# Moving one block of VectorE work and splitting one exponential in a fused attention and feed-forward kernel

## The chip, the cores and the metric

The kernel runs on one core of a Trainium2 chip. The metric is device time in microseconds (us); of each kernel several executions are timed and the median is given. One execution is recorded by the hardware profiler; its rows are what the text quotes. The engines are TensorE (PE in the profile, its weight loads PEld), VectorE (DVE), ScalarE (ACT), GpSimd (POOL) and SyncE (SP). SP issues most transfers between memory and the chip's buffers, among them transfers that transpose. Every engine works through its own instructions in order and waits on semaphores for those of the others.

## The reference

Inputs are `x` (8 batches, 8 heads, 512 positions, 64 wide), `state` (8, 8, 32, 64) and two matrices, 512 by 2048 and 2048 by 512. For each batch and head:

```python
scores  = x @ state.T / 8;   a  = softmax(scores)      # over 32 states
xread   = a @ state
scores2 = state @ x.T / 8;   a2 = softmax(scores2)     # over 512 positions
sread   = a2 @ x
attn    = concat([xread, sread])                        # 544 rows
h = attn (all heads side by side, 4352 rows of 512) @ w_in
out = max(0.01 * h, h) @ w_out
```

The sums of both softmaxes get 1e-9 added. Input and output are fp32.

## The kernel before

**Tiling.** The kernel goes batch by batch, 0 to 7. All eight heads of a batch are one tile: the scores stand as 128 partitions (4 pairs of heads times 32 states) by 2 times 512 positions, in a PSUM tile of two banks called "sc". Most products run on bf16 copies. Instead of `a @ state @ w_in` the kernel forms `M = state @ w_in` once per batch, in four column blocks (`a_m(a, c, tag)` makes block c on PE in the PSUM tile named by `tag`, `m_evict` copies it to `a.M`), so that the first feed-forward layer is one product of the probabilities with M.

**A batch's first softmax** on the engines: `a_scores` (PE), then on DVE `a_max` (L266, maximum over the 32 states) and the two steps of `a_diff`: the maxima are spread over a tile `sh` (L274) and the scores less the maxima overwrite it (L280). `a_exp` (ACT, L284) writes the exponentials to `e1`. `a_recip` (DVE: L289 sums, L293 and L296 give the reciprocal, L298 spreads it) and `a_probs` (L302) give the probabilities `aT`.

**The second softmax** of the same scores: `a_max2` (DVE, L331), `a_exp2` (ACT, L337, for each half g, with the sums collected on the way in `r2`), `a_probs2` (DVE: L345 adds 1e-9, L347 the reciprocal, L355 two multiplications to bf16, one for each half). For batches 0 and 1 the result goes into a common tile `a2p`; a transfer on SP transposes it (`a_a2t_pair`, L373), and `a_sread` on PE multiplies it with x later, in batch 2's stage.

**The feed-forward layers.** `ff1(a, hT, s)`, s from 0 to 15, is a step: two matmuls into a bank of the tag "ph" (two banks in turn), then relu s on ACT (L437). A step's bank is free again for step s + 2 once relu s is done. The second layer of a batch runs as `piece`s between the steps: for batches 0 and 1 `piece(b, hT, i, jq)` adds four matmuls to the output block i, `y_store` (L547) copies a finished block out of PSUM with ACT or DVE and sends it off by SP (L548). From batch 1's second half on, products are replaced by sums of blocks and fewer products (a Strassen-like scheme): `tw_sum` forms combinations of w_out (L576), `s_sum` (L597) and `two_sum` (L673) those of h; `two_product` (L689, tile `ppr`) and `product` (L632) multiply.

**Order.** The order on every engine is written out by hand; the program text is the order of issue. The loop `for s in range(16)` with `ff1(a1, h1, s)` is batch 1's stage. Before it stands a prologue with batch 0's rest: there `a_exp2(a0)` is issued, `a_scores(a1)`, `a_shift(a1)` (maximum, spread, subtraction), `a_max2(a1)`, `a_exp(a1)`, the casts and transposing transfers of x for batch 2 (`cast_x`, L126, and `a_xt_half`, L240), the probabilities of batch 1, the cast and transposing transfer of the state for batches 2 and 3 (L209, L214), two `tw_sum`s of DVE (with `j` 0 and 4), `a_probs2(a0)`, and eight `tw_sum`s and a cast on POOL.

Two output blocks of batch 0 (i = 2 and 3) stand in a two-bank PSUM tile, `pyw`, of the tag "big". In step 1 of batch 1's stage their last matmuls run, and ACT copies block 2 and DVE block 3. In step 3, after `a_scores(a2)`, `a_m(a1, 3, "big")` writes into the same two banks (`pm`, L411), ACT evicts it, and DVE does `a_shift(a2)` and `a_max2(a2)`. In step 7 `a_exp(a2)` follows relu 7 on ACT; in step 9 `a_exp2(a2, 0)` follows relu 9, and on DVE come `a_recip(a2)` and `a_probs(a2)`; in step 11 `a_exp2(a2, 1)` and `a_probs2(a2)`; in step 13 `a_probs2(a1)`, an eviction of M of batch 2 by DVE (L425) and four `two_sum`s, with two more in step 0 of batch 2's stage. In step 1 of batch 2's stage `m_spread` (L1113) evicts one block of M from two banks, "ph" with ACT and "py" with DVE; the first `two_product` in step 2 takes that "py" bank after it.

Of the kernel before, what the change touches and what calls it, by code (L numbers as in the profile page):

```python
# [9 lines left out]
P = 128  # L10
B, H, S, D = 8, 8, 512, 64
# [8 lines left out]
BF16 = mybir.dt.bfloat16  # L20
FP32 = mybir.dt.float32
AF = mybir.ActivationFunctionType
ALU = mybir.AluOpType
# [4 lines left out]
def kernel(  # L28
# [9 lines left out]
    nc = tc.nc  # L38
# [4 lines left out]
    att = ctx.enter_context(tc.tile_pool(name="att", bufs=2))  # L43
# [10 lines left out]
    NB = 2 * S // NS  # L54
# [144 lines left out]
    def load_state(i):  # L199
        lo, hi = groups[i]  # L200
        for k in range(NK):
            for g in range(2):
                nc.sync.dma_start(
                    stf[i][NS * k:NS * (k + 1), :, D * g:D * (g + 1)],
                    state[lo:hi, 2 * k + g].rearrange("b n d -> n b d"),
                )
# [45 lines left out]
    def a_scores(a):  # L252
        sc = psum.tile([P, 2, S], FP32, name="sc", tag="sc", bufs=1)
        for k in range(NK):
            for g in range(2):
                nc.tensor.matmul(
                    sc[NS * k:NS * (k + 1), g, :],
                    lhsT=st_of(a, g, k),
                    rhs=a.xTh[k // 2][D * g:D * (g + 1), :, k % 2, :],
                    start=True, stop=True,  # L260
                )
        a.sc = sc

    def block_max(flat, n):
        m1 = att.tile([P, n], FP32, name="mrow", tag="mrow")
        nc.vector.tensor_reduce(  # L266
            out=m1[:], in_=flat.rearrange("p (c j) -> p c j", j=NS),
            axis=AX.X, op=ALU.max, apply_transpose=True,
        )
        return m1  # L270

    def block_spread(m1, n):
        sh = att.tile([P, n * NS], FP32, name="sh", tag="sh", bufs=1)
        nc.vector.transpose(  # L274
            sh[:].rearrange("p (c j) -> p c j", j=NS), m1[:, :, None].to_broadcast([P, n, NS])
        )
        return sh

    def block_diff(flat, sh):
        nc.vector.tensor_tensor(out=sh[:], in0=flat, in1=sh[:], op=ALU.subtract)  # L280

    def block_exp(sh, n):
        e1 = att.tile([P, n * NS], BF16, name="e1", tag="e1", bufs=1)
        nc.scalar.activation(out=e1[:], in_=sh[:], func=AF.Exp)  # L284
        return e1
# [21 lines left out]
    def a_max(a):  # L307
        a.flat = a.sc[:].rearrange("p g c -> p (g c)")
        a.m1 = block_max(a.flat, NB)

    def a_diff(a):
        a.sh = block_spread(a.m1, NB)
        block_diff(a.flat, a.sh)

    def a_shift(a):
        a_max(a)
        a_diff(a)

    def a_exp(a):
        a.e1 = block_exp(a.sh, NB)  # L320

    def a_recip(a):
        a.q1b = block_recip(a.e1, NB)

    def a_probs(a):
        a.aT = att.tile([P, 2, S], BF16, name="aT", tag="aT")
        block_probs(a.aT[:], a.e1, a.q1b)

    def a_max2(a):
        a.m2 = att.tile([P, 2], FP32, name="mcol", tag="mcol")  # L330
        nc.vector.tensor_reduce(out=a.m2[:], in_=a.sc[:], axis=AX.X, op=ALU.max, negate=True)  # L331

    def a_exp2(a, g):
        if g == 0:
            a.e2 = att.tile([P, 2, S], BF16, name="e2", tag="e2")
            a.r2 = att.tile([P, 2], FP32, name="r2", tag="r2")
        nc.scalar.activation(  # L337
            out=a.e2[:, g], in_=a.sc[:, g, :], func=AF.Exp,
            bias=a.m2[:, g:g + 1], accum_out=a.r2[:, g:g + 1],
        )  # L340
# [3 lines left out]
    def a_probs2(a):  # L344
        nc.vector.tensor_scalar(out=a.r2[:], in0=a.r2[:], scalar1=1e-9, scalar2=None, op0=ALU.add)  # L345
        q2 = att.tile([P, 2], FP32, name="qc", tag="qc")
        nc.vector.reciprocal(q2[:], a.r2[:])  # L347
        if a.b in (0, 6):
            pairs[a.b] = att.tile([P, 2, 2, S], BF16, name="a2p", tag="a2p", bufs=1)
        if a.b in (0, 1, 6, 7):  # L350
            a.a2 = pairs[a.b - a.b % 2][:, a.b % 2]
        else:
            a.a2 = att.tile([P, 2, S], BF16, name="a2", tag="a2", bufs=1)[:]
        for g in range(2):
            nc.vector.tensor_scalar(  # L355
                out=a.a2[:, g, :], in0=a.e2[:, g, :],
                scalar1=q2[:, g:g + 1], scalar2=None, op0=ALU.mult,
            )
# [60 lines left out]
    def m_evict(a, c, pm, copy):  # L419
        cols = slice(DM * c, DM * (c + 1))  # L420
        if isinstance(pm, list):
            for g in range(2):
                copy(a.M[:, g, cols], pm[g][:])
        else:
            copy(a.M[:, :, cols], pm[:])  # L425
# [3 lines left out]
    def ff1(a, hT, j):  # L429
        ph = psum.tile([P, S], FP32, name="ph", tag="ph")  # L430
        for g in range(2):
            nc.tensor.matmul(  # L432
                ph[:], lhsT=a.M[:, g, P * j:P * (j + 1)],
                rhs=a.aT[:, g, :],
                start=(g == 0), stop=(g == 1),
            )
        nc.scalar.activation(out=hT[:, j, :], in_=ph[:], func=AF.Prelu, scale=1 / SCALE, alpha=0.01)  # L437
# [93 lines left out]
    def piece(b, hT, i, jq, bank=None, copy=SCA, js=range(4)):  # L531
        if jq == 0 and js[0] == 0:
            y = ys[b, i] = Y()
            y.py = psum.tile([P, DM], FP32, name="py", tag="py")[:] if bank is None else bank
        y = ys[b, i]
        for j in [4 * jq + v for v in js]:
            nc.tensor.matmul(  # L537
                y.py, lhsT=hT[:, j, P * i:P * (i + 1)], rhs=w_out_bf[:, j, :],
                start=(j == 0), stop=(j == 15),
            )  # L540
        if jq == 3 and copy is not None:
            y_store(b, i, copy)

    def y_store(b, i, copy):
        tag = ("ysb", "s1", "ysb", "s6")[i]
        ysb = ypool.tile([P, DM], FP32, name="ysb", tag=tag, bufs=3 if tag == "ysb" else 1)
        copy(ysb[:], ys[b, i].py)  # L547
        nc.sync.dma_start(rows_of(b)[i], ysb[:])  # L548
# [18 lines left out]
    def tw_sum(n, j0, j1, eng):  # L567
        u, at = j0 // 4, slice(j0 % 4, j0 % 4 + j1 - j0)
        in0, in1 = {
            1: lambda: (w_block(0, 1, j0, j1), w_block(0, 0, j0, j1)),  # L570
            2: lambda: (w_block(1, 1, j0, j1), tw[1][u][:, at]),
            3: lambda: (w_block(1, 1, j0, j1), w_block(0, 1, j0, j1)),
            4: lambda: (w_block(1, 0, j0, j1), tw[2][u][:, at]),
        }[n]()
        with nc.allow_low_precision(reason="operands of bf16 products"):
            eng.tensor_tensor(out=tw[n][u][:, at], in0=in0, in1=in1, op=ALU.subtract)  # L576
# [185 lines left out]
    a0, a1, a2 = att_of[:3]  # L762
# [249 lines left out]
    m_evict(a1, 1, a_m(a1, 1, "ph"), SCA)  # L1012
    for i in (0, 1):
        piece(0, h0, i, 0, js=half[1])
    a_shift(a1)
    a_max2(a1)
    tw_open()
# [25 lines left out]
        piece(0, h0, i, 3, copy=None, js=half[0])  # L1043
    for j in (0, 4):
        tw_sum(2, j, j + 4, nc.vector)
    a_probs2(a0)
    for n in (4, 3):
        for j in range(0, HJ, 2):
            tw_sum(n, j, j + 2, nc.gpsimd)
# [6 lines left out]
    for s in range(16):  # L1056
        ff1(a1, h1, s)
        if s in (1, 3):
            two = ((2, SCA), (3, VEC)) if s == 1 else ((0, SCA), (1, SCA))
            for i, copy in two:  # L1060
                piece(0, h0, i, 3, copy=None, js=half[1])
            for i, copy in two:
                y_store(0, i, copy)
        elif s % 2:
            piece(*fill[s // 2 - 2])
        if s == 3:
            a_scores(a2)
            m_evict(a1, 3, a_m(a1, 3, "big"), SCA)
            a_shift(a2)
            a_max2(a2)  # L1070
        elif s == 5:
            load_state(1)
        elif s == 7:
            a_exp(a2)
            a_open(att_of[3], 3)
            a_xt_dma(att_of[3])
        elif s in (9, 11):
            a_exp2(a2, s // 2 - 4)
            if s == 9:
                a_a2t_pair(0, (0,))  # L1080
                a_recip(a2)
                a_probs(a2)
            else:
                a_probs2(a2)
                load_x(4, nc.sync)
        elif s == 13:
            a_probs2(a1)
            a_a2t_pair(0, (1,))
            pm = [a_m(a2, 0, "big"), a_m(a2, 1, "sc")]
            m_evict(a2, 0, pm[0], SCA)  # L1090
            m_evict(a2, 1, pm[1], VEC)
            q1 = two_open(h1, 2 * P, ("S0", "S1"), "py")
            for n in (1, 2, 3):
                two_sum(q1, n, 0, 4, nc.vector)
            two_sum(q1, 3, 4, 8, nc.vector)
# [19 lines left out]
    for b in range(2, B):  # L1115
        hT = hpool.tile([P, 16, S], BF16, name="hT", tag="hT")
        hTs[b] = hT
        a = att_of[b]
# [192 lines left out]
```

## Time and profile before

| | us |
|---|---|
| median of 3 runs (203.39 to 203.48) | 203.41 |
| the profiled execution | 203.55 |
| its span in the profile | 201.8 |
| PE busy | 193.9 (96%) |
| DVE busy | 161.8 (80%) |
| ACT busy | 142.0 (70%) |
| POOL busy | 72.7 (36%) |

The clock that PE was granted is full throughout. The first number of a timeline row is its start in us from the span's start, the second its length; then come engine, source line, operation, output and input tile, the count if several are merged, and in brackets how long the engine had been idle before and what ended that. `PEld` is PE's weight load, `SPq` is SP's queue. Ends of matmuls are modelled, so rows of PE overlap a little; starts are what can be compared. In the table of groups a row has line, engine, operation, tiles and shapes, count, then total busy us and mean ns.

### The profile page before, as it was taken

The page shows a single profiled execution, that of the slowest core. Times are in us where ns is not written, and L with a number is a line of the kernel's source. Part 1 is how long each engine was busy: PE and PEld are TensorE (multiplying, and loading weights), DVE is VectorE, ACT ScalarE, POOL GpSimd, SP SyncE. Part 2 cuts the span into 40 slices and gives each one's busy share as a digit, 9 for nine tenths or more (in the row PEclk, how much of TensorE's full clock was granted, in tenths as well). Part 3 has the DMA queues.
Part 4 walks back from the last instruction along what each step waited for, and adds up shares of the span by engine and source line. Part 5 has one row for each costly group of instructions (what it writes and reads, how often), then busy time and mean ns, then how long its engine had stood idle before and what let it go on. Part 6 is the DMA issues. An engine that isn't in the chain of part 4 may idle for free.

```text
span 201.8 us, 4599 instructions
## 1 busy us (share of the span) xinstructions
PE 193.9 (96%) x1853; PEld 129.9 (64%) x1880; DVE 161.8 (80%) x240; ACT 142.0 (70%) x273; POOL 72.7 (36%) x76
## 2 busy tenths in 40 slices
PE   7899999799999999999999999999999999999993
PEld 3543444344477667776776767676767777799982
DVE  2766798999998989985999889898999945984712
ACT  3579647788889868866887779686868555757420
POOL 8914184990280274027400670054004600540000
PEclk9999999999999999999999999999999999999999
DMA  5999999697999723952382505220025302210115
GB/s 200 208 207 298 210 292 154 150 355 152 241 218 160 279 54 50 234 239 55 71 241 110 157 3 104 104 109 0 0 89 164 61 3 99 112 45 12 52 38 170
DMA packets 38773, 27.75 MB, mean 138 GB/s; under 512 B 24416, under 2 KB 35808, under 8 KB 38752
## 3 DMA queue, kind: packets, MB, share of 16 engines
q1 hardware_dynamic: 33584, 20.78, 38.7%
q0 software_dynamic: 4832, 6.29, 15.3%
q10 hardware_dynamic: 336, 0.39, 0.8%
q8 instruction: 14, 0.23, 0.5%
q14 instruction: 7, 0.06, 0.1%
HBM read 17.30 MB, written 8.91 MB: 130 GB/s over the span
## 4 chain that ended last, share of the span: by engine, by line
PE 76%; DMA 15%; POOL 3%; DVE 3%; issue 1%; ACTq 1%; ACT 0%; POOLq 0%; DVEq 0%
PE ph L432 21%; PE ppx L632 18%; PE ppb L632 15%; DMA x<-in_x_dram 7%; DMA w_out_bf<-in_moe_w_out_dram 7%; PE ppr L689 6%; PE pm L411 3%; PE py L537 3%; PE pf L510 3%; PE ppw L632 3%; PE psr L384 2%; POOL w_in_bf L145 2%; DVE a2p L355 1%; DMA out_dram<-ysb 1%; DVE tw L576 1%
## 5 line engine op out<-in xcount | busy, mean ns | idle before, releaser
L437 ACT ACTIVATE hT<-ph 128x512 bf16<-128x512 f32 x112 | 66.5, 604 | 24.8 <-PE ph L432 21.8
L597 POOL TENSOR_TENSOR S<-hT,S 128x512 bf16<-128x512 bf16 x24 | 32.1, 1358 | 83.2 <-DVE S L597 68.3
L432 PE MATMUL ph<-aT,M 128*128 128x512 bf16 x202 | 60.6, 379 | 0.1
L632 PEld LDWEIGHTS <-S 128*128 128x128 bf16 x384 | 37.0, 98 | 12.7 <-issue 0.9
L632 PEld LDWEIGHTS <-hT 128*128 128x128 bf16 x288 | 28.0, 98 | 11.1
L597 DVE TENSOR_TENSOR S<-hT 128x1024 bf16<-128x1024 bf16 x24 | 24.8, 1056 | 3.6 <-ACT hT L437 3.5
L432 PEld LDWEIGHTS <-M 128*128 128x128 bf16 x224 | 20.9, 98 | 8.4 <-issue 2.3
L632 PE MATMUL ppx<-tw,S 128*128 128x256 bf16 x160 | 20.8, 273 | 0.3
L537 PEld LDWEIGHTS <-hT 128*128 128x128 bf16 x96 | 9.1, 97 | 11.4 <-issue 1.1
L537 PE MATMUL py<-w_out_bf,hT 128*128 128x512 bf16 x61 | 15.7, 379 | 0.1
L729 DVE TENSOR_TENSOR ysb<-ppb,s 128x512 f32<-128x512 f32 x12 | 8.3, 692 | 6.5 <-PE ppb L632 6.5
L632 PE MATMUL ppb<-w_out_bf,hT 128*128 128x256 bf16 x96 | 12.4, 273 | 0.2
L632 PE MATMUL ppb<-tw,S 128*128 128x256 bf16 x96 | 12.4, 272 | 0.1
L632 PE MATMUL ppb<-w_out_bf,S 128*128 128x256 bf16 x96 | 12.3, 273 | 0.2
L425 ACT CAST M<-pm 128x1024 bf16<-128x1024 f32 x11 | 11.2, 1018 | 1.7 <-PE pm L411 1.7
L632 PE MATMUL ppx<-w_out_bf,hT 128*128 128x256 bf16 x80 | 11.2, 272 | 0.1
L337 ACT ACTIVATE e<-sc,mcol 128x512 bf16<-128x512 f32 x16 | 11.1, 701 | 0.0
L632 PE MATMUL ppx<-tw,hT 128*128 128x256 bf16 x80 | 10.4, 273 | 0.2
L576 POOL TENSOR_TENSOR tw<-w_out_bf 128x512 bf16<-128x512 bf16 x8 | 9.0, 1161 | 4.0 <-DMA w_out_bf<-in_moe_w_out_dram 4.0
L132 POOL CAST xb<-xl 128x2048 bf16<-128x2048 f32 x5 | 9.5, 1893 | 0.8 <-PE psr L384 0.8
L331 DVE TENSOR_REDUCE mcol<-sc 128x2 f32<-128x1024 f32 x8 | 9.7, 1213 | 0.0
L289 DVE TRANSPOSE_TENSOR_REDUCE r<-e 128x32 f32<-128x1024 bf16 x7 | 8.7, 1245 | 1.0 <-ACT e L284 0.7
(147 smaller groups left out, 324.7 us busy)
## 6 DMA issues: line engine op xcount, KB each, us to landing
out_dram<-ysb SPq DMA_DIRECT2D x11, 512.0 KB, 2.7
xl<-in_x_dram SPq DMA_DIRECT2D x5, 1024.0 KB, 6.1
out_dram<-ysb SPq DMA_DIRECT2D x9, 256.0 KB, 4.5
w_in_bf<-in_moe_w_in_dram POOLq DMA_DIRECT2D x4, 512.0 KB, 9.1
xf<-in_x_dram SPq DMA_DIRECT2D x4, 256.0 KB, 3.8
w_out_bf<-in_moe_w_out_dram POOLq DMA_DIRECT2D x4, 256.0 KB, 13.6
x<-in_x_dram POOLq DMA_DIRECT2D x2, 512.0 KB, 14.4
w_out_bf<-in_moe_w_out_dram POOLq DMA_DIRECT2D x2, 512.0 KB, 16.8
```

The lines of the kernel that those rows point to most:

```text
L132: nc.gpsimd.tensor_copy(xt[b][:].rearrange("p t h d -> p h t d"), xl[b][:].rearrange("p h (t d) -> p h t d", t=NT),)
L289: nc.vector.tensor_reduce(out=r1[:], in_=e1[:].rearrange("p (c j) -> p c j", j=NS), axis=AX.X, op=ALU.add, apply_transpose=True,)
L331: nc.vector.tensor_reduce(out=a.m2[:], in_=a.sc[:], axis=AX.X, op=ALU.max, negate=True)
L337: nc.scalar.activation(out=a.e2[:, g], in_=a.sc[:, g, :], func=AF.Exp, bias=a.m2[:, g:g + 1], accum_out=a.r2[:, g:g + 1],)
L425: copy(a.M[:, :, cols], pm[:])
L432: nc.tensor.matmul(ph[:], lhsT=a.M[:, g, P * j:P * (j + 1)], rhs=a.aT[:, g, :], start=(g == 0), stop=(g == 1),)
L437: nc.scalar.activation(out=hT[:, j, :], in_=ph[:], func=AF.Prelu, scale=1 / SCALE, alpha=0.01)
L537: nc.tensor.matmul(y.py, lhsT=hT[:, j, P * i:P * (i + 1)], rhs=w_out_bf[:, j, :], start=(j == 0), stop=(j == 15),)
L576: eng.tensor_tensor(out=tw[n][u][:, at], in0=in0, in1=in1, op=ALU.subtract)
L597: eng.tensor_tensor(out=part(n), in0=in0, in1=in1, op=op)
L632: nc.tensor.matmul(q[bank][v], lhsT=lhsT, rhs=w_of(n, j), start=q["open", bank] and j == 0, stop=j == 7, skip_group_check=True,)
L689: nc.tensor.matmul(q.bank[w], lhsT=lhsT, rhs=w_of(n, j), start=n in (1, 2, 5) and j == 0, stop=j == HJ - 1, skip_group_check=True,)
```

## The change

Two things are altered. First, `a_probs2(a0)` (four DVE instructions) is issued ahead of `a_shift(a1)` in the prologue instead of behind the two DVE `tw_sum`s. Second, in batch 1's stage `a_shift(a2)` becomes `a_max(a2)` and `a_diff_halves(a2)`: the subtraction is issued as two instructions, one for each half of 512 columns; and `a_exp(a2)` becomes two instructions of 512 columns, of which the first stays behind relu 7 and the second goes behind relu 9, ahead of `a_exp2(a2, 0)`. The numbers computed are the same.

```diff
     def block_diff(flat, sh):
-        nc.vector.tensor_tensor(out=sh[:], in0=flat, in1=sh[:], op=ALU.subtract)
+        nc.vector.tensor_tensor(out=sh, in0=flat, in1=sh, op=ALU.subtract)
...
+    def a_diff_halves(a):
+        a.sh = block_spread(a.m1, NB)
+        a.e1 = att.tile([P, 2 * S], BF16, name="e1", tag="e1", bufs=1)
+        for g in range(2):
+            block_diff(a.flat[:, S * g:S * (g + 1)], a.sh[:, S * g:S * (g + 1)])
+
+    def a_exp_half(a, g):
+        at = slice(S * g, S * (g + 1))
+        nc.scalar.activation(out=a.e1[:, at], in_=a.sh[:, at], func=AF.Exp)
...
     for i in (0, 1):
         piece(0, h0, i, 0, js=half[1])
+    a_probs2(a0)
     a_shift(a1)
     a_max2(a1)
...
     for j in (0, 4):
         tw_sum(2, j, j + 4, nc.vector)
-    a_probs2(a0)
     for n in (4, 3):
...
         if s == 3:
             a_scores(a2)
             m_evict(a1, 3, a_m(a1, 3, "big"), SCA)
-            a_shift(a2)
+            a_max(a2)
+            a_diff_halves(a2)
             a_max2(a2)
         elif s == 5:
             load_state(1)
         elif s == 7:
-            a_exp(a2)
+            a_exp_half(a2, 0)
             a_open(att_of[3], 3)
             a_xt_dma(att_of[3])
         elif s in (9, 11):
+            if s == 9:
+                a_exp_half(a2, 1)
             a_exp2(a2, s // 2 - 4)
```

More of the change, by code (lines that the diff above doesn't have):

```diff
@@ L312, in a_diff @@
         a.sh = block_spread(a.m1, NB)
-        block_diff(a.flat, a.sh)
+        block_diff(a.flat, a.sh[:])
     def a_shift(a):
```

## The prediction

> **What bounds the kernel now.** I read the page's busy table first, then the chain of work that ended last in order of time, then the timeline around the places that the change touches.
>
> ```profile
> PE 193.9 (96%) x1853; PEld 129.9 (64%) x1880; DVE 161.8 (80%) x240; ACT 142.0 (70%) x273; POOL 72.7 (36%) x76
> ```
>
> TensorE (PE) works 193.9 us, 96% of the span of 201.8. So the question for each edit is whether it opens or closes one of the few holes in PE's time. The profiled execution took 203.55 us, 1.75 outside its span; the median of the three runs is 203.41, so what the sum moves is taken off 203.41. In the chain, from 34.87 us:
>
> ```profile
> 34.87 1.27 DVE tw L576
> 36.14 1.05 DVE r L345
> 37.41 2.17 DVE a2p L355 x2
> 39.58 0.61 DVE ysb L547
> ```
>
> From 36.1 to 39.6 the chain runs through `a_probs2(a0)` on VectorE (DVE): add, reciprocal, two multiplications. Behind it on the same queue stands a copy of a finished output block out of PSUM (L547, `y_store(0, 3, VEC)`). The timeline shows who waits for that copy:
>
> ```profile
> 34.44 4.99 POOL L576 TENSOR_TENSOR tw<-w_out_bf,tw 128x512 bf16<-128x512 bf16 x4 [1.18 <-DVE tw L576]
> ...
> 35.64 1.18 SPq L214 DMA_TRANSPOSE st_t<-stb  x1
> ...
> 36.98 0.59 ACT L547 COPY ysb<-pyw 128x512 f32<-128x512 f32 x1 [0.21 <-PE pyw L537]
> ...
> 38.43 1.09 ACT L547 COPY ysb<-py 128x512 f32<-128x512 f32 x2
> 38.72 0.11 PEld L256 LDWEIGHTS <-st_t 64*32 64x32 bf16 x8 [0.55 <-DMA st_t<-stb]
> ...
> 39.50 0.68 DVE L547 COPY ysb<-pyw 128x512 f32<-128x512 f32 x1
> ...
> 40.23 0.41 PE L411 MATMUL pm<-w_in_bf,st 64*32 64x512 bf16 x8 [1.10 <-DVE ysb L547]
> ```
>
> PE finishes the scores of batch 2 (L256) and stands 1.10 us, until the copy has emptied the two-bank "big" tile that `a_m(a1, 3, "big")` writes. It is PE's one long hole behind the start.
>
> **Part 1, the block leaves its old place.** The copy needs the product of its rows, and is queued until ScalarE (ACT) has copied its sister block: 36.98 + 0.59 = 37.57. With the block gone DVE ends the second `tw_sum` at 34.87 + 1.27 = 36.14 and is free. The copy then runs from 37.6 to 38.3 (0.68 by its row), before PE arrives. On SP its output transfer, and the state loads queued behind that, go earlier by as much; their readers are a stage away. The block itself issues no transfer. What is late next is the scores themselves: they start when the transposed state has landed.
>
> ```profile
> DMA to landing us min/median/max: 3.0/3.0/3.0
> ```
>
> 35.64 + 3.0 = 38.64, the scores at 38.72; nothing in the change moves this transfer (next part). After the scores, `a_m` can follow as it does one stage later, where no one is waited for:
>
> ```profile
> 53.67 0.40 PE L256 MATMUL sc<-xT,st_t 64*32 64x512 bf16 x8
> 53.88 0.40 PE L411 MATMUL pm<-w_in_bf,st_t 64*32 64x512 bf16 x8
> ...
> 55.52 1.04 PE L689 MATMUL ppr<-w_out_bf,hT 128*128 128x256 bf16 x8
> ```
>
> That is 0.21 after the scores' start, so 38.93 instead of 40.23: PE gains 1.30. ACT's next work, the eviction of this product, comes free at about 39.45 (two copies from 38.43); it began 0.48 after `a_m`'s start before (40.71, below) and would be ready at 39.41. I take PE's lead as D = 1.25.
>
> **Part 1, the block at its new place.** It stands now behind the copies of x^T (L1008) and ahead of batch 1's maximum (L266).
>
> ```profile
> 23.05 1.40 DVE L1008 COPY xT<-pxt 128x1024 bf16<-128x1024 bf16 x2
> ...
> 23.21 0.25 ACT L337 ACTIVATION_READ_ACCUMULATOR e<-sc,mcol 128x1 f32 x1
> ...
> 24.51 0.41 PE L256 MATMUL sc<-xT,st 64*32 64x512 bf16 x8
> ...
> 24.99 1.25 DVE L266 TRANSPOSE_TENSOR_REDUCE mrow<-sc 128x32 f32<-128x1024 f32 x1 [0.55 <-PE sc L256]
> ...
> 26.11 4.50 POOL L576 TENSOR_TENSOR tw<-w_out_bf 128x512 bf16<-128x512 bf16 x4 [4.04 <-DMA w_out_bf<-in_moe_w_out_dram]
> ...
> 33.07 0.69 DVE L302 TENSOR_TENSOR aT<-e,qb 128x1024 bf16<-128x1024 bf16 x1
> 33.23 1.04 ACT L126 CAST xb<-xl 128x1024 bf16<-128x1024 f32 x1 [1.45 <-DMA xl<-in_x_dram]
> ...
> 35.05 1.03 PE L432 MATMUL ph<-aT,M 128*128 128x512 bf16 x4
> ```
>
> Its input is ready: the last exponential of batch 0 ends at 23.46. Price, from the two such blocks that stand back to back later:
>
> ```profile
> 48.83 0.16 DVE L345 TENSOR_SCALAR r<-r 128x2 f32<-128x2 f32 x1
> ...
> 49.76 0.16 DVE L345 TENSOR_SCALAR r<-r 128x2 f32<-128x2 f32 x1
> ```
>
> 49.76 - 48.83 = 0.93. DVE is free at 24.45 and has 0.55 of idle time, so the maximum moves from 24.99 to 25.4, 0.4 late. Queued behind it: batch 1's subtraction, exponential and sum. ACT's exponential and next eviction move 0.4, and the first cast of x for batch 2 with them, and its transpose on SP; the second cast waits anyway for its transfer (1.45 us before 33.23), and SP's second transpose and the state transpose behind it go by that one. The probabilities of batch 1 (L302) end at 33.76, then at 34.2; PE reads them at 35.05. The second `tw_sum` waited for a weight transfer until 34.87 and takes up the rest. POOL starts its sums (34.44) 0.3 later, but has no multiplications of DVE between them any more, which I count as even. Cost on PE: 0. The cover is 1.2 us wide; without it each 0.1 us costs 0.1.
>
> Here a rule can be weighed. At the old place the same block took from 36.06 to 39.50, 3.44 us, the add 1.05 instead of 0.16. POOL's sums ran all that time, and at the new place POOL is idle until 26.11. If the slowness travelled with the block, batch 1's maximum would come 2.9 late, its probabilities at 36.7, PE would stand 1.6 at 35.05, and D would be 1.25 - 1.6 = -0.35. The Trainium skill, "SBUF — State Buffer", section "Who interferes with whom", says that VectorE and GpSimd share a pair of ports under an exclusive lock and the one that comes second is blocked outright, and that a scalar multiplication out of SBUF may take that pair. By that rule the block costs 0.93 here, and the sum stays; by the other reading it is the last rival but one.
>
> **Part 2, two halves.** Around the exponential of batch 2 (all as before the change):
>
> ```profile
> 40.71 1.01 ACT L425 CAST M<-pm 128x1024 bf16<-128x1024 f32 x1 [1.18 <-PE pm L411]
> ...
> 42.31 1.04 PE L432 MATMUL ph<-aT,M 128*128 128x512 bf16 x4
> 42.65 1.22 DVE L280 TENSOR_TENSOR sh<-sc,sh 128x1024 f32<-128x1024 f32 x1
> 42.94 1.08 ACT L437 ACTIVATE hT<-ph 128x512 bf16<-128x512 f32 x2 [0.23 <-PE ph L432]
> ...
> 43.79 1.21 DVE L331 TENSOR_REDUCE mcol<-sc 128x2 f32<-128x1024 f32 x1
> ...
> 43.97 1.06 ACT L284 ACTIVATE e<-sh 128x1024 bf16<-128x1024 f32 x1
> 44.05 1.03 PE L432 MATMUL ph<-aT,M 128*128 128x512 bf16 x3
> ...
> 44.94 1.07 ACT L437 ACTIVATE hT<-ph 128x512 bf16<-128x512 f32 x2
> 45.06 1.25 DVE L289 TRANSPOSE_TENSOR_REDUCE r<-e 128x32 f32<-128x1024 bf16 x1
> ...
> 45.89 0.69 ACT L337 ACTIVATE e<-sc,mcol 128x512 bf16<-128x512 f32 x1
> ```
>
> DVE's chain started with batch 2's maximum, queued behind the copy (39.50 + 0.68). Freed of it, it goes by the scores: 38.72 + 0.48 (batch 1: scores at 24.51, maximum at 24.99) = 39.2, 0.9 earlier. Subtraction in halves: 1.22 for the whole; the nearest half-size row is DVE's copy out of PSUM at 0.68, so 1.22 to 1.36, ending near 43.0 (maximum and transpose take 2.55: 42.65 less 40.10, where the copy had ended); the row maxima (L331, 1.21) end near 44.2. Both halves are there before ACT wants them.
>
> The exponential is the costly part. Before, it ran whole ahead of relu 8 (43.97 to 45.03) and DVE's sum L289 followed at 45.06. Now only half is ahead, and the sum waits for the half that is behind relu 9. Size of a half, by the other exponential of 128x512:
>
> ```profile
> L337 ACT ACTIVATE e<-sc,mcol 128x512 bf16<-128x512 f32 x16 | 11.1, 701 | 0.0
> ...
> L836 ACT ACTIVATE e<-scn 128x512 bf16<-128x512 f32 x2 | 1.2, 597 | 1.6 <-PE scn L810 1.6
> ```
>
> ACT starts work every 0.49 when it has a queue (two relus from 44.94, next start 45.89: 0.48 each; 42.94 to 43.97: 0.51). Relu 8 needs its product: PE starts it at 44.05 - D, and a relu begins 0.63 after its product's start (42.31, 42.94, where ACT was idle). So relu 8 at 44.68 - D, relu 9 0.49 later, half 1 another 0.49 later, 0.60 long, and the sum 0.03 after it: 46.29 - D. With D = 1.25 that is 45.04: DVE's sum starts no earlier than before (45.06), though PE is 1.25 ahead, and DVE stands idle from 44.2 to 45.0. Relus 10 and 11 come about 0.3 late against PE, which has 0.3 to 0.4 to spare there (an estimate: relu 10 came behind the exponential of 45.89, near 46.55, and its bank is wanted again two steps of 1.74 us, 42.31 to 44.05, after 44.05, near 47.5); at most 0.1 is lost, and the next step has room for it.
>
> Now DVE's queue behind the sum, which ran without a hole before:
>
> ```profile
> 53.74 0.43 DVE L673 TENSOR_TENSOR Sr<-Sr,hT 128x512 bf16<-128x512 bf16 x1
> 54.38 0.69 DVE L1113 CAST M<-pm 128x512 bf16<-128x512 f32 x1 [0.22 <-PE pm L411]
> ```
>
> From 45.06 to 54.17 DVE is busy end to end (probabilities of batch 2, two second-probability blocks, an eviction, six sums); then 0.22 idle, then the eviction of its half of `m_spread` (L1113). PE's first product ppr (55.52) reuses that "py" bank and, by the program's semaphores, waits for this eviction. Before: 54.38 + 0.69 = 55.07, 0.40 to spare (0.05 for the signal). Now the eviction starts at 54.20 + (46.29 - D - 45.06) and PE goes on 0.74 later: 56.17 - D. So PE keeps 55.52 - (56.17 - D) = D - 0.65. With D = 1.25: **0.60 us**; the other 0.65 is a new stall of PE at L689. After that PE leads by 0.60 and DVE by about 0.2 or less; I expect DVE to catch up within batch 2's relus and the stages behind, where PE sets the pace (96% busy), to keep the 0.60. 203.41 - 0.60 = 202.8.
>
> Unknown sizes: half 1 between 0.49 (a start each) and 0.70 (the exponential L337 with its sum, 701 ns), the relus' rhythm 0.48 to 0.55, D 1.15 to 1.30: the gain is 0.35 to 0.80, my value by the rows nearest in form.
>
> **Rivals.**
> 1. The backlog doesn't bind: DVE finds 0.5 us or more in the nine behind the sum, or the sum starts earlier. Then PE keeps the whole D: 203.41 - 1.25 = 202.15. For it: PE's and ACT's lead brings the inputs of these nine earlier. Against it: none of them waited for an input before, so earlier inputs shorten nothing.
> 2. The hole closes only partly, because the copy is itself held by POOL's sums. If it lost 0.94 like the add did, it ends at 39.25, D = 0.95 and the gain is 0.30: 203.1, no change. Against: its row has 0.68 though POOL's sum ran at that time. The Trainium skill's "SBUF — State Buffer" page, same section, agrees: an instruction with at most one SBUF input outside the two-port modes doesn't take the pair.
> 3. Slower: the block keeps its 3.44 us at the new place. D = -0.35, gain -1.0: 204.4. It decides from a block of about 1.7 us on (0.55 idle and 1.2 cover). Against it: POOL idle, and 0.93 at 48.83.
> 4. The removal does nothing, as another wait (ACT's sister copy, the transfer) holds `a_m` until 40.2. D = 0, and the halves cost 0.65: 204.05. It is slower by more than 0.41 from D under 0.24 on.
>
> **How the numbers follow.** 0.2% is 0.41 us, about what a measurement of this kernel can tell from no change. Forecast (gain 0.35 to 0.80, so 202.6 to 203.05): 0.60, of which 0.09 under 0.41. Rival 1: 0.14. Rival 2 and other partial losses down to nothing: 0.14. Rivals 3 and 4: 0.06 each. Faster 0.51 + 0.14 = 0.65, same 0.09 + 0.14 = 0.23, slower 0.12. The range goes from rival 1 to no gain, 202.1 to 203.5; it leaves out the slower rivals.
>
> **What would show it.** PE's wait for L547 at 40 us gone, `a_m` right behind the scores near 38.9; the moved block about 0.93 us long at 24.4; batch 1's ff1 at 35.05 as before; DVE idle near 44.5 until half 1's end near 45.0; a new wait of PE for M L1113 of some 0.5 us near 54.4; POOL's sums at 34 to 39 shorter. Wrong if PE waits at 35 us (rival 3), if the hole stays (4), or if no wait at L689 appears (1).

## The result

The changed kernel takes 202.74 us (median of 7) against 203.39 us for the kernel before on the same chip (7 runs): a ratio of 0.9973, 95% interval 0.9961 to 0.9986. The forecast was 202.8, a gain of 0.60; the medians differ by 0.65. The ratio, which leaves out one slower execution of 207.68 us, puts the gain at 0.55, between 0.28 and 0.79. The profiled execution took 202.80, its span is 201.0 instead of 201.8.

The changed file is longer, so line numbers behind the change are shifted by about ten: relus are L447, steps of `ff1` L442, `a_m` L421, the output copy L557, `two_product` L699, `m_spread` L1126, the halves of the exponential L330.

The busy table of the page:

```profile
PE 194.4 (97%) x1853; PEld 130.3 (65%) x1880; DVE 159.9 (80%) x241; ACT 142.3 (71%) x274; POOL 72.6 (36%) x76
```

PE runs the same 1853 matmuls. Its busy time is 0.5 us longer, nearly all of it ahead of batch 1's scores (22.75 against 22.30); behind them, up to the first `two_product`, its idle time shrinks. The view of who PE waited for, from 24 to 62 us, has no line for the output copy any more (1.1 us before). One line is new:

```profile
PE ppr L699 <- DVE M L1126: 0.4, 1, 0.4
```

The timeline of the changed kernel at the places that the prediction followed (start, length, engine, line):

```profile
24.31 0.16 DVE L355 TENSOR_SCALAR r<-r 128x2 f32<-128x2 f32 x1
...
24.46 0.41 PE L256 MATMUL sc<-xT,st 64*32 64x512 bf16 x8
...
24.71 0.62 DVE L365 TENSOR_SCALAR a2p<-e,qc 128x512 bf16<-128x512 bf16 x2
...
25.24 1.24 DVE L266 TRANSPOSE_TENSOR_REDUCE mrow<-sc 128x32 f32<-128x1024 f32 x1
...
33.31 0.69 DVE L302 TENSOR_TENSOR aT<-e,qb 128x1024 bf16<-128x1024 bf16 x1
...
35.00 1.03 PE L442 MATMUL ph<-aT,M 128*128 128x512 bf16 x4
...
37.55 0.69 DVE L557 COPY ysb<-pyw 128x512 f32<-128x512 f32 x1 [1.16 <-ACT ysb L557]
...
38.64 0.41 PE L256 MATMUL sc<-xT,st_t 64*32 64x512 bf16 x8
...
38.87 0.40 PE L421 MATMUL pm<-w_in_bf,st 64*32 64x512 bf16 x8
...
42.55 0.62 ACT L330 ACTIVATE e<-sh 128x512 bf16<-128x512 f32 x1
42.72 1.03 PE L442 MATMUL ph<-aT,M 128*128 128x512 bf16 x3
...
44.33 0.63 ACT L330 ACTIVATE e<-sh 128x512 bf16<-128x512 f32 x1
...
44.99 1.25 DVE L289 TRANSPOSE_TENSOR_REDUCE r<-e 128x32 f32<-128x1024 bf16 x1 [0.88 <-ACT e L330]
...
53.67 0.42 DVE L683 TENSOR_TENSOR Sr<-Sr,hT 128x512 bf16<-128x512 bf16 x1
...
54.01 0.68 DVE L1126 CAST M<-pm 128x512 bf16<-128x512 f32 x1
...
54.75 1.03 PE L699 MATMUL ppr<-w_out_bf,hT 128*128 128x256 bf16 x8 [0.35 <-DVE M L1126]
```

The moved block runs from 24.31 to the next start at 25.24: 0.93 us instead of 3.44. PE reads batch 1's probabilities at 35.00 without a wait. The copy L557 is done at 38.24, and `a_m` follows the scores by 0.23 instead of 1.51. DVE's sum L289 nevertheless starts at 44.99, where it started before (45.06), 0.88 us idle in front of it, and at 54.75 PE meets the new wait, for DVE's half of `m_spread`.

All profiles begin with a stretch of loading that differs by up to 1.2 us between executions. To compare spans without it I take the time from batch 1's scores (the row at 24.46; 24.51 before) to the start of the last run of products. The chain of the changed kernel and of the one before end with these products:

```profile
188.21 6.13 PE ppr L699 x56
```

```profile
188.98 6.13 PE ppr L689 x56
```

188.21 - 24.46 = 163.75 against 188.98 - 24.51 = 164.47: 0.72 less. To the first ppr it is 54.75 - 24.46 = 30.29 against 31.01, also 0.72 less. So the whole gain is what is won at 39 us less what is lost at 54, and the 130 us behind keep it.

### The profile page after: what moved, and what is told of

Its sections match the earlier page's. It is cut to its first block, busy times and chain, and to the rows that moved or that the text cites. A ratio compares the mean times of both kernels' runs of the same rounds, so it can differ in the third digit from the quotient of the medians.

```text
span 201.0 us, 4601 instructions
## 1 busy us (share of the span) xinstructions
PE 194.4 (97%) x1853; PEld 130.3 (65%) x1880; DVE 159.9 (80%) x241; ACT 142.3 (71%) x274; POOL 72.6 (36%) x76
## 4 chain that ended last, share of the span: by engine, by line
PE 79%; DMA 8%; DVE 5%; POOL 3%; ACT 1%; issue 1%; ACTq 1%; POOLq 0%
PE ph L442 20%; PE ppx L642 18%; PE ppb L642 15%; DMA x<-in_x_dram 7%; PE ppr L699 6%; PE py L547 3%; PE pf L520 3%; PE pm L421 3%; PE pyw L547 3%; PE ppw L642 3%; PE psr L394 2%; POOL w_in_bf L145 2%; DVE Sr L683 1%; DMA out_dram<-ysb 1%; PE sc L256 1%
## 5 line engine op out<-in xcount | busy, mean ns | idle before, releaser
L447 ACT ACTIVATE hT<-ph 128x512 bf16<-128x512 f32 x112 | 66.6, 605 | 25.1 <-PE ph L442 22.1
L442 PE MATMUL ph<-aT,M 128*128 128x512 bf16 x202 | 60.7, 379 | 0.1
L442 PEld LDWEIGHTS <-M 128*128 128x128 bf16 x224 | 20.9, 98 | 8.7 <-issue 2.9
L289 DVE TRANSPOSE_TENSOR_REDUCE r<-e 128x32 f32<-128x1024 bf16 x7 | 8.7, 1245 | 1.4 <-ACT e L330 0.9
```

Of the source, the lines that this page charges most:

```text
L289: nc.vector.tensor_reduce(out=r1[:], in_=e1[:].rearrange("p (c j) -> p c j", j=NS), axis=AX.X, op=ALU.add, apply_transpose=True,)
L442: nc.tensor.matmul(ph[:], lhsT=a.M[:, g, P * j:P * (j + 1)], rhs=a.aT[:, g, :], start=(g == 0), stop=(g == 1),)
```

## The experiments

Each row of the table is a profile; "to ppr" is the start of the first `two_product` and "to the end" that of the last run of products, both counted from batch 1's scores. "Sum" is the start of DVE's sum L289, counted alike.

| kernel | sum | to ppr | to the end | against before | median, us (before on that chip) |
|---|---|---|---|---|---|
| before | 20.55 | 31.01 | 164.47 | | 203.41 |
| changed | 20.53 | 30.29 | 163.75 | -0.72 | 202.74 (203.39) |
| changed, again | 20.60 | 30.36 | 163.82 | -0.65 | 202.86 (203.42) |
| e1 move only | 19.65 | 29.94 | 163.41 | -1.06 | 202.44 (203.49) |
| e2 halves only | 21.82 | 31.58 | 165.04 | +0.57 | 204.17 (203.49) |
| e3 both halves behind relu 7 | 19.57 | 29.86 | 163.32 | -1.15 | 202.44 (203.49) |
| e4 two sums behind the subtraction | 20.68 | 29.92 | 164.79 | +0.32 | 203.86 (203.49) |
| e6 block under POOL's sums | 21.46 | 31.58 | 165.04 | +0.57 | 204.09 (203.42) |
| e7 two sums behind the maxima | 20.54 | 29.78 | 163.24 | -1.23 | 202.07 (203.42) |
| e7, again | 20.63 | 29.87 | 163.33 | -1.14 | 202.40 (203.43) |
| e8 second half behind relu 8 | 20.05 | 29.86 | 163.33 | -1.14 | 202.45 (203.42) |
| e9 whole exponential behind relu 9 | 21.10 | 30.85 | 164.32 | -0.15 | 203.17 (203.43) |
| e10 move and two sums, no halves | 19.77 | 30.06 | 163.53 | -0.94 | 202.46 (203.43) |

Two executions of the same kernel differ by 0.07 to 0.09 in this count, so steps of a tenth say nothing. Part of such a difference is the start of batch 2's scores, which wait for their transposed state: it lies 14.10 to 14.37 behind batch 1's in these profiles (15.02 in e6, where PE itself is late). The intervals of e2, e4 and e9 contain 1, so their times alone do not tell them from the kernel before; what is said of them rests on the traces.

### One part at a time: e1 and e2

e1 is the kernel before with the block moved and nothing else:

```diff
+    a_probs2(a0)
     a_shift(a1)
...
         tw_sum(2, j, j + 4, nc.vector)
-    a_probs2(a0)
```

> The block of second probabilities moved, nothing split. My theory (PE keeps its lead D less what DVE's queue behind the sum L289 lacks, and the halves only delay that sum): the whole exponential ends near 44.0, the sum starts near 44.1 instead of 45.0, DVE's half of m_spread ends 0.9 earlier, PE does not wait at its first ppr; relus 8 and 9 come 0.5 late and cost PE 0.1. Gain 1.1 to 1.2 against before: 202.2 to 202.3. Rival A (ACT binds: the whole exponential in front of relus 8 and 9 holds PE's steps 10 and 11 by 0.4 or more, which is what the split is for): 202.6 to 202.8, with a wait of PE for ph near 44.5. Rival B (the move alone is the whole effect and the split does nothing): same as the changed kernel, 202.7.

Measured: 202.44, ratio 0.9947 (0.9921 to 0.9974). The move alone gains more than the whole change, 1.06 against 0.72 in the count from batch 1's scores; the intervals of the two ratios overlap a little. Its timeline:

```profile
42.82 1.06 ACT L284 ACTIVATE e<-sh 128x1024 bf16<-128x1024 f32 x1 [0.26 <-DVE sh L280]
...
43.48 1.03 PE L537 MATMUL py<-w_out_bf,hT 128*128 128x512 bf16 x4
...
43.91 1.25 DVE L289 TRANSPOSE_TENSOR_REDUCE r<-e 128x32 f32<-128x1024 bf16 x1
43.96 1.89 POOL L132 CAST xb<-xl 128x2048 bf16<-128x2048 f32 x1
...
44.41 1.08 PE L432 MATMUL ph<-aT,M 128*128 128x512 bf16 x4
...
45.18 0.70 DVE L293 TENSOR_SCALAR r<-r 128x32 f32<-128x32 f32 x1
...
51.98 1.09 DVE L673 TENSOR_TENSOR Sr<-hT 128x512 bf16<-128x512 bf16 x3
...
53.45 0.68 DVE L1113 CAST M<-pm 128x512 bf16<-128x512 f32 x1
...
54.20 1.04 PE L689 MATMUL ppr<-w_out_bf,hT 128*128 128x256 bf16 x8
```

The exponential runs whole behind relu 7 and DVE's sum starts at 43.91, 0.9 earlier than in the changed kernel counted from the scores (19.65 against 20.53). PE does not wait at ppr: it starts at 54.20, 0.43 behind the row before it, as in the kernel before (55.52 - 55.09). It is a close thing, as DVE's half of `m_spread` ends only at 54.13. Rival A falls: PE's step at 44.41, which needs relu 8, comes 0.93 behind the row before it instead of 0.86, a loss of about 0.1 as the theory had it and not of 0.4. What I had not seen: of the 0.9 us half is lost again, as the small addition L293 behind the sum takes 0.70 instead of 0.18 while POOL's cast (43.96 to 45.85) runs.

e2 is the changed kernel with `a_probs2(a0)` back behind the two `tw_sum`s.

> The block at its old place, the subtraction and the exponential in halves. My theory: the hole of 1.1 us at 40 stays, the sum L289 starts near 46.3 instead of 45.06, DVE's half of m_spread ends near 56.1 and PE waits about 0.6 at its first ppr: slower by 0.65, 204.05. Rival (the split is free, as DVE catches up elsewhere): 203.4.

```profile
40.52 0.41 PE L421 MATMUL pm<-w_in_bf,st 64*32 64x512 bf16 x8 [1.02 <-DVE ysb L557]
...
46.61 1.25 DVE L289 TRANSPOSE_TENSOR_REDUCE r<-e 128x32 f32<-128x1024 bf16 x1 [1.25 <-ACT e L330]
...
56.37 1.03 PE L699 MATMUL ppr<-w_out_bf,hT 128*128 128x256 bf16 x8 [0.35 <-DVE M L1126]
```

Measured: 204.17, ratio 1.0024 (0.9999 to 1.005); 0.57 more from scores to the end, with 0.65 foretold. Both waits of PE stand in it, 1.02 before `a_m` and 0.35 before ppr. The interval touches 1, so on times alone it would be unclear; the trace shows the sum 1.27 later and the ppr 0.57 later than before.

### Is it the split or its place: e3, e8, e9

Three variants of the changed kernel move only the exponential: e3 issues both halves behind relu 7, e8 the second half behind relu 8, e9 the whole as one instruction behind relu 9.

```diff
 e3:         elif s == 7:
             a_exp_half(a2, 0)
+            a_exp_half(a2, 1)
...
-            if s == 9:
-                a_exp_half(a2, 1)
```

```diff
 e8:
+        elif s == 8:
+            a_exp_half(a2, 1)
         elif s in (9, 11):
-            if s == 9:
-                a_exp_half(a2, 1)
```

```diff
 e9:         elif s == 7:
-            a_exp_half(a2, 0)
...
             if s == 9:
-                a_exp_half(a2, 1)
+                nc.scalar.activation(out=a2.e1[:], in_=a2.sh[:], func=AF.Exp)
```

> The changed kernel with the second half of the exponential directly behind the first, both behind relu 7. It tells the cost of splitting from the cost of the place. My theory: the place is all of it; as with the move alone, the sum starts near 44.1, no wait at ppr, 202.2 to 202.4. Rival (two instructions cost as such): 202.6 to 202.8.

> The changed kernel with the second half of the exponential behind relu 8 instead of relu 9. Theory: DVE's sum L289 starts 0.5 earlier (near 44.5), but of that POOL's cast (to 45.9) may hold the small addition L293 by 0.1 to 0.2, so DVE's half of m_spread ends 0.3 to 0.4 earlier, PE's wait at ppr shrinks from 0.52 (against its step) to 0.1 to 0.2: gain 1.0, about 202.4 if before is 203.4. Rival (the wait does not follow the second half): 202.7.

> The changed kernel with the whole exponential as one instruction behind relu 9 (nothing of it ahead). It asks what the first half, left in front, is worth. Theory: the sum L289 starts 0.43 later than in the changed kernel (a whole takes 1.06, a half 0.63), near 45.4; PE is first held a little by relu 10, and then at ppr 0.43 longer; gain 0.29 instead of 0.72 between batch 1's scores and the last products, 203.1 to 203.2. Rival (DVE makes up for it): 202.8.

Measured: e3 202.44, ratio 0.9947 (0.9928 to 0.9967); e8 202.45, 0.9955 (0.9942 to 0.9968); e9 203.17, 0.9988 (0.9967 to 1.001). From e8 and e9:

```profile
43.69 0.62 ACT L330 ACTIVATE e<-sh 128x512 bf16<-128x512 f32 x1
...
44.34 1.25 DVE L289 TRANSPOSE_TENSOR_REDUCE r<-e 128x32 f32<-128x1024 bf16 x1 [0.49 <-ACT e L330]
...
54.15 1.04 PE L699 MATMUL ppr<-w_out_bf,hT 128*128 128x256 bf16 x8
```

```profile
44.30 1.06 ACT L1089 ACTIVATE e<-sh 128x1024 bf16<-128x1024 f32 x1
...
45.39 1.25 DVE L289 TRANSPOSE_TENSOR_REDUCE r<-e 128x32 f32<-128x1024 bf16 x1 [1.27 <-ACT e L1089]
...
46.56 1.08 PE L442 MATMUL ph<-aT,M 128*128 128x512 bf16 x4 [0.25 <-ACT hT L447]
...
55.14 1.03 PE L699 MATMUL ppr<-w_out_bf,hT 128*128 128x256 bf16 x8 [0.35 <-DVE M L1125]
```

In order of the sum's start (19.57, 20.05, 20.53, 21.10 for e3, e8, changed, e9) the time to ppr is 29.86, 29.86, 30.29, 30.85: once the sum starts later than about 20.1, a delay of the sum by 0.48 and by 0.57 more costs PE 0.43 and 0.56 at ppr. Earlier than that it buys nothing, for two reasons. In e3 the gain is lost in DVE's queue, as L293 behind the sum takes 0.73 under POOL's cast:

```profile
45.62 0.73 DVE L293 TENSOR_SCALAR r<-r 128x32 f32<-128x32 f32 x1
```

DVE's half of `m_spread` starts 29.13 behind batch 1's scores in e3 and 29.08 in e8. And PE then comes to ppr at its own step or nearly so, 0.46 (e3) and 0.43 (e8) behind the row before it. Two instructions instead of one cost nothing that is seen (e3 and e1: 163.32 and 163.41). e8 did a little better than I had expected: no wait was left. e9 did a little worse (0.15 gained, 0.29 expected), as the sum came 0.57 later and not 0.43. Of that, 0.18 is batch 2's scores, which began 14.36 behind batch 1's instead of 14.18, with the landing of their transposed state; counted from them the sum is 0.39 later. PE was also held by relu 10, 0.25 before the step at 46.56, but that costs nothing more, as it waited for DVE at ppr all the same.

### Is the wait at ppr DVE's backlog: e4, e7, e10

The place stays as in the changed kernel, but two of the six sums in DVE's queue ahead of `m_spread`, those with n = 3, which a later product reads, go behind it. e4 puts them behind batch 3's subtraction, e7 behind its row maxima:

```diff
-            for n in (1, 2, 3):
+            for n in (1, 2):
                 two_sum(q1, n, 0, 4, nc.vector)
-            two_sum(q1, 3, 4, 8, nc.vector)
...
 e4:             a_shift(nxt)
                 if b > 2:
                     a_max2(nxt)
+                else:
+                    for j in (0, 4):
+                        two_sum(q1, 3, j, j + 4, nc.vector)
...
 e7:         elif s == 3 and b == 2:
                 a_max2(nxt)
+                for j in (0, 4):
+                    two_sum(q1, 3, j, j + 4, nc.vector)
```

> The changed kernel, halves and places as they are, but the two sums n = 3 of DVE (2 times 0.36 us, needed only by a product four us later) go from the front of DVE's half of m_spread to behind batch 3's subtraction. If PE's wait at its first ppr is DVE's backlog, as I say, that half ends 0.7 earlier, the wait of PE (0.5 late against its step) goes, and PE keeps D: 202.1 to 202.25. Rival (what holds PE there is something else, or the wait turns up again at the next reader): 202.6 to 202.75.

Measured: 203.86, ratio 1.0013 (0.9985 to 1.004), and a miss for the expected time. The timeline shows why:

```profile
53.57 0.68 DVE L1125 CAST M<-pm 128x512 bf16<-128x512 f32 x1
...
54.46 1.04 PE L699 MATMUL ppr<-w_out_bf,hT 128*128 128x256 bf16 x8
...
57.77 1.89 POOL L132 CAST xb<-xl 128x2048 bf16<-128x2048 f32 x1 [0.24 <-PE psr L394]
57.86 2.41 DVE L683 TENSOR_TENSOR Sr<-hT 128x512 bf16<-128x512 bf16 x2
...
60.20 0.41 DVE L709 TENSOR_TENSOR ysb<-ppr,rkept 128x256 f32<-128x256 f32 x1
...
60.66 1.05 PE L699 MATMUL ppr<-tw,Sr 128*128 128x256 bf16 x8 [1.23 <-DVE ysb L709]
```

The wait at the first ppr is gone (54.46 is 1.09 nearer to the scores than before). But the two sums start under POOL's cast and take 2.41 us together, the first of them 2.08; three such sums take 1.09 where POOL is idle (the row at 51.98 in e1's profile). The addition L709 behind them starts at 60.20, and PE waits 1.23 for it at a later ppr. The Trainium skill, "SBUF — State Buffer", section "Who interferes with whom", says that a VectorE instruction with both inputs in SBUF contends with a GpSimd instruction that reads SBUF. By that rule the first sum waits for the cast, and the trace agrees: the cast ends at 57.77 + 1.89 = 59.66, the first sum 0.28 behind it and the second at 60.27.

> As the run with the two sums n = 3 taken out of the way of DVE's half of m_spread, but put behind batch 3's row maxima L341 (near 59.9), where POOL's cast of 58.05 to 59.95 is over, instead of ahead of them. Theory (the wait at the first ppr is DVE's backlog, and the run before lost its gain to the collision with the cast): no wait at ppr for M and none for L709 at 60.7, the sums 0.36 each, gain against before 1.1 to 1.25, 202.2 to 202.4. Rival (moving them costs as such, the next reader waits anyway): 203 or more.

```profile
44.75 1.25 DVE L289 TRANSPOSE_TENSOR_REDUCE r<-e 128x32 f32<-128x1024 bf16 x1 [0.86 <-ACT e L330]
...
53.10 0.68 DVE L1125 CAST M<-pm 128x512 bf16<-128x512 f32 x1
...
53.99 1.04 PE L699 MATMUL ppr<-w_out_bf,hT 128*128 128x256 bf16 x8
...
57.30 1.89 POOL L132 CAST xb<-xl 128x2048 bf16<-128x2048 f32 x1 [0.24 <-PE psr L394]
...
58.86 0.95 DVE L683 TENSOR_TENSOR Sr<-hT 128x512 bf16<-128x512 bf16 x2
```

Measured: 202.07, ratio 0.9951 (0.9931 to 0.997); a second time, beside e10:

> The kernel with the sums n = 3 behind batch 3's row maxima once more, beside the next: 0.9935 to 0.995 of before, 202.1 to 202.3.

202.40, ratio 0.9943 (0.9922 to 0.9963). No wait at either ppr. The sums did not come behind the cast as expected, but 0.33 before its end (59.19), as the row maxima ran earlier too; they took 0.95 together, at no cost to PE. So the wait at ppr was DVE's backlog: with 0.7 us less in the queue it is gone with the halves left where they are, and with the sum starting where it does in the changed kernel (20.54).

e10 has the block moved and the two sums as in e7, but nothing split:

> The block moved and the sums n = 3 moved, but nothing split. Theory: once PE's wait at ppr is gone by either means, the split has no more to give, and the other means nothing to add: 1.1 to 1.25 less than before between batch 1's scores and the last products, as with the split, 202.1 to 202.4. If the whole exponential in front of relu 8 costs PE more than 0.1, it is slower than the kernel beside it by so much.

202.46, ratio 0.9964 (0.9947 to 0.9981); 0.94 less in the count from the scores, where 1.1 to 1.25 were expected. DVE has room now, as its half of `m_spread` waits for PE:

```profile
53.33 0.69 DVE L1112 CAST M<-pm 128x512 bf16<-128x512 f32 x1 [0.46 <-PE pm L411]
```

What is missing was lost before that. Batch 2's scores began 14.31 behind batch 1's, 0.10 later than in the first e7. And relu 8 stands behind the whole exponential: PE's step that needs it starts at 44.68, 1.06 behind the row before it, where e7 has 0.87 (44.21 - 43.34). From batch 2's scores to ppr it is 15.75 in e10, as in e1, and 15.57 and 15.68 in the two profiles of e7. So the split may be worth one or two tenths in this company; the times (202.46 against 202.40 in the same comparison) can't tell.

### The price of the block: e6

The changed kernel with the block one place later, behind batch 1's subtraction, where POOL's sums run:

```diff
-    a_probs2(a0)
     a_shift(a1)
+    a_probs2(a0)
     a_max2(a1)
```

> The changed kernel with the moved block one place later, behind batch 1's subtraction (near 29.0) instead of ahead of its maximum: there POOL's four sums of 26.1 to 30.6 are running. If the block's price at its old place came from POOL (my theory), it takes about 2.2 us here instead of 0.93 and ends only when POOL's sums do, near 31.2; batch 1's sum L289 starts near 32.4 instead of 30.15, its probabilities end near 36.2, PE waits 1.2 to 1.3 at ff1 of step 0 (35.0), the lead D is used up and the time is 203.9 to 204.2. If the block's price was its own at the old place and POOL has no part in it (rival), it takes 0.93, the probabilities end at 34.9, PE does not wait, 202.7.

```profile
26.05 4.50 POOL L586 TENSOR_TENSOR tw<-w_out_bf 128x512 bf16<-128x512 bf16 x4 [4.05 <-DMA w_out_bf<-in_moe_w_out_dram]
...
28.64 0.81 DVE L355 TENSOR_SCALAR r<-r 128x2 f32<-128x2 f32 x1
...
29.49 0.17 DVE L357 RECIPROCAL qc<-r 128x2 f32<-128x2 f32 x1
29.69 1.26 DVE L365 TENSOR_SCALAR a2p<-e,qc 128x512 bf16<-128x512 bf16 x2
...
30.88 1.21 DVE L341 TENSOR_REDUCE mcol<-sc 128x2 f32<-128x1024 f32 x1
...
35.16 0.69 DVE L302 TENSOR_TENSOR aT<-e,qb 128x1024 bf16<-128x1024 bf16 x1
...
35.91 1.04 PE L442 MATMUL ph<-aT,M 128*128 128x512 bf16 x4 [0.97 <-DVE aT L302]
```

Measured: 204.09, ratio 1.0033 (1.0021 to 1.0045). From 28.64 to the next start at 30.88 the block takes 2.24 us. The addition ends at 29.45 and the first multiplication at 30.69, just behind two of POOL's sums (29.44 and 30.55); the second multiplication meets no sum any more and takes 0.34. At the old place all three end like that, 0.02 to 0.15 behind a sum. PE waits 0.97 for the probabilities at 35.91, where 1.2 to 1.3 were expected, and 0.72 again at ppr. That is 0.37 more than in the changed kernel, by which L293, here under POOL's cast, is longer (0.55 instead of 0.18). The same four instructions thus cost 0.93, 2.24 or 3.44 us by what POOL does meanwhile.

### The changed kernel again

> The changed kernel itself, to stand on the same chip beside the next three. As measured first: 0.997 of before; from batch 1's scores to the last run of products 0.72 less than before, one wait of PE at ppr for M, 0.35.

202.86, ratio 0.9969 (0.9955 to 0.9983), with the same wait. e7 is 0.8 us below it in the same comparison. Which of e1, e3, e7 and e8 is the fastest the runs can't tell: their ratios lie between 0.9943 and 0.9955, within each other's intervals.

## Why the prediction was right, step by step

- **The hole before `a_m` closes, D = 1.25.** `a_m` started 0.23 behind the scores (0.21 foretold, 1.51 before), 1.28 won. At relu 8's product the lead, counted from batch 2's scores, is (44.05 - 38.72) - (42.72 - 38.64) = 1.25. The rest went where the working put it, to ACT's queue: step 7, near 41.4, is 0.04 late behind relu 5, which stands behind the eviction in ACT's queue and ends at 41.38. Rival 4 is out, and rival 2 as well: the copy took 0.69 with POOL's sums beside it. DVE's second `tw_sum` came later than foretold (35.16, again waiting for its weights, instead of 34.87), which DVE's idle 1.16 us ahead of the copy covers.
- **The block costs 0.93 and hides.** It took 0.93. Batch 1's maximum starts 0.78 behind the scores instead of 0.48, so 0.30 late (0.4 foretold); the probabilities end at 34.0 and PE started its step at 35.00. Rival 3 is out here, and e6 shows that it was a question of the place: beside POOL's sums the block is slow at its new place too, though it takes 2.24 there and not 3.44.
- **The halves hold DVE's sum at its old start.** Foretold 45.04 against 45.06; measured 44.99. A half took 0.62 to 0.63 (0.60 taken).
- **DVE's queue carries that to `m_spread` and PE.** PE kept 0.72 where the working gave 0.60. The difference is one term: from the sum L289 to the last sum of the queue it is 8.68 us in both kernels (53.74 - 45.06 and 53.67 - 44.99), but I let the eviction start 0.46 behind that last sum's start (54.20 - 53.74), just after its row ends, and it started 0.34 behind it (54.01 - 53.67). Rival 1 is out, and e3, e7 and e8 show what PE keeps where the queue doesn't bind: 1.14 to 1.23, near the 1.25 of that rival.
- **The stages behind keep it.** 0.72 at ppr, 0.72 at the end. The trace thus gives 0.72, the medians 0.65 and the ratio 0.55; with two executions 0.07 to 0.09 apart, how close 0.60 comes to each of them says little, and the steps above say more.
- **Not seen:** that DVE starts earlier only to meet POOL's cast (e1's L293, 0.70). My working let every tenth by which the sum starts earlier reach `m_spread`; in e1 only 0.36 of 0.88 does. It made little difference to the time, as PE comes to ppr at its own step by then.
- **A sign that failed.** POOL's sums at 34 to 39 were to become shorter without the block between them. They took 4.94 us instead of 4.99. They start 0.30 later, counted from batch 1's scores, as foretold, and the next four 0.25 later, which had been counted as even. No wait of PE follows from it.

The two parts of the change thus work against each other: the move is worth 1.06 to 1.15, the place of the second half takes 0.4 of it back, and alone it costs 0.57.

## What to carry to other kernels

When a hole of the bounding engine closes, ask of every queue that feeds it later by how much it runs ahead: the lead that the engine wins is only kept as far as those queues move too, and here one instruction issued two relus too late kept DVE at its old time. Look for the queue's longest stretch without idle time and the last row in it that someone waits for; taking 0.7 us out of that stretch was worth as much as the better place of the exponential. Before a VectorE block is moved, read what GpSimd does at both places: the same block cost 0.93, 2.24 and 3.44 us.

## What the runs showed of the hardware that was not expected

- A VectorE addition on 128x32 fp32 numbers took 0.70 instead of 0.18 us when it came while GpSimd's cast of 128x2048 was running (e1, 45.18), and ended just behind that cast (45.85). In e3, e6 and e10 it took 0.73, 0.55 and 0.44 and ended 0.04 to 0.05 behind the cast. In e8 it came at 45.62, just before the cast's end (45.66), and took 0.18. The reciprocal of 128x2 in the moved block took 0.17 everywhere, also beside a running sum of GpSimd (e6, 29.49).
- Two VectorE sums of 128x512 bf16 took 2.41 us under such a cast (e4), 0.95 in e7 where they began 0.33 before its end, and 0.36 each where GpSimd was idle. In e4 and e7 the first of them ended 0.28 behind the cast.
- The maximum and the subtraction out of PSUM and the transposing sum were not slowed by GpSimd. In the kernel before, the maximum took 1.23 and the subtraction 1.22 with POOL's sums running (40.10, 42.65), 1.25 and 1.22 with POOL idle (24.99, 78.54); the transposing sum took 1.25 under the cast (e1, 43.91) and with POOL idle (before, 80.94).
